# Attention of three more batches on 64x64 quarters of the array, with two casts moved ahead of value loads

## Chip, cores and metric

The kernel runs on one core of one Trainium2 chip. The metric is the time of one execution on the device in microseconds (us), median of several runs. A profile's span runs from the first to the last instruction and is some 1.7 us shorter than that run's time.

## The reference, cut to what matters

```python
# q, k, v: (8 batches, 8 heads, 576 tokens, 64), fp32
q_d, k_d, v_d = means of four neighbouring tokens          # 144 coarse tokens
out_d     = softmax(q_d k_d^T / 8) v_d, repeated 4 times
out_local = softmax(q k^T / 8 where |i - j| < 4) v         # a narrow band
x = (out_up + out_local) as (4608 tokens, 512)
h = x @ w_in                    # 512 -> 2048
return gelu(h) @ w_out          # 2048 -> 512
```

The two dense layers (called MoE here) run in nine blocks of 512 tokens. While block c runs, the attention of batch c+1 is woven into it, so that the matmuls of the layers fill the time in which attention waits for exponentials.

## The kernel before

Attention has two forms. `attn` uses the whole 128x128 array, with keys and values of two heads laid out in zero-padded blocks; it served batches 1 to 5. `attn_q` uses the array as four 64x64 quarters; it served batches 6 and 7. `BQ` is the first batch on quarters. `fill(n)` issues n matmuls of the dense layers. Cuts are marked.

```python
    BQ = 6
    ...
    def scores(b, p):                     # whole array: 12 matmuls for a pair of heads
        for hh in range(2):
            nc.tensor.matmul(out=sc[...144 wide], lhsT=kdz[:, p, hh, 0:128], rhs=qd[:, p, :], ...)
        for j in range(NW):               # NW = 10 windows
            nc.tensor.matmul(out=sc[...57 to 60 wide], lhsT=kb[:, p, j, :], rhs=(qT0 if b == 1 else xT_of(b, "qn"))[...], ...)
    ...
    def scores_q(b, p):                   # quarters: 28 matmuls for a pair of heads
        for c in range(2):
            for hh in range(2):
                for g in range(2):
                    nc.tensor.matmul(out=sc[HS[g], o:o + DH], lhsT=kdt[HS[hh], p, HS[c]],
                                     rhs=qd[HS[hh], p, DH * g:DH * g + DH], start=True, stop=True)
        for i in range(5):
            for hh in range(2):
                for g in range(2):
                    nc.tensor.matmul(out=sc[HS[g], o:o + RL[i]], lhsT=kt[HS[hh], p, k0:k0 + 64],
                                     rhs=qt[HS[hh], p, q0:q0 + RL[i]], start=True, stop=True)
    ...
    def prep_q(b):                        # VectorE, for quarters
        if b == BQ:
            ...                           # masks and constants, once
        nc.vector.tensor_reduce(out=kdt, in_=kt...)           # sums of the keys
        nc.vector.tensor_reduce(out=qd, in_=qt...)            # sums of the queries
        ...                               # 8 copies of coarse keys into KE
        v_two(...); v_two(...); v_two(...)                    # sums of the values
        ...                               # 4 copies into v_d, 4 products into v_lm
    def attn_q(b, fill):
        fill(5)
        s_lo_q(b); scores_q(b, 0); exps_q(0)
        fill(11)
        for p in range(NP):               # NP = 4 pairs of heads
            av_q(b, p)
            if p + 1 < NP:
                scores_q(b, p + 1)
            norm_qa(p)
            ...
            else:
                fill(12)
    ...
    for c in range(NCH):                  # 9 blocks
        b = c + 1
        ...
        (prep_q if b >= BQ else prep)(b)
        ...
        f1()
        if b < B:
            (attn_q if b >= BQ else attn)(b, f2)
            if 1 < b < B - 2:
                v_load(b + 2)             # GpSimd: values, for two batches on
            if 1 < b < B - 3:
                qk_cast(b + 3)            # GpSimd: keys and queries to fp16 in DRAM
        f2()
        if 1 < b < B - 2:
            qk_turn(b + 2)                # SP: transposes from DRAM into SBUF
```

What the argument turns on stands between the lines: for every pair of heads a quarter form issues one burst of 76 small matmuls (28 of scores and 48 of averages), each with a weight load of its own (436 and 437 recorded for 438 matmuls in the stages of batches 6 and 7), and then 12 long matmuls of the dense layers.

## Time and profile before

| | before |
|---|---|
| median time | 323.03 us (321.87 to 323.53, 3 runs) |
| span of the profiled run | 321.2 us |
| TensorE busy | 98% of the span, 2850 matmuls |
| stage of batch 3 / 4 / 5 (whole array) | 33.43 / 32.69 / 32.70 us |
| stage of batch 6 / 7 (quarters) | 31.98 / 31.99 us |

A "stage" runs from the first matmul of a block to the first of the next, and I name it after the batch whose attention is in it.

### The profile page before, as it was taken

How to read it: one execution, taken by the hardware profiler on the slowest of the kernel's cores; microseconds unless marked ns; L12 is line 12 of the kernel's file. 1: busy time of each engine (PE TensorE's matmuls, PEld its weight loads, DVE VectorE, ACT ScalarE, POOL GpSimd, SP SyncE). 2: the span in 40 equal slices, each digit the busy share in tenths (PEclk: the TensorE clock that was granted, in tenths of full speed). 3: DMA queues.
4: the chain of work that ended last, by engine and by line, in shares of the span. 5: the costliest groups of instructions: out<-in, count | busy, mean ns of one | idle time of the engine just before them, and what ended most of it. 6: DMA issues, size and time to landing. Idle time of an engine off the chain costs nothing.

```text
span 321.2 us, 6933 instructions
## 1 busy us (share of the span) xinstructions
PE 313.4 (98%) x2850; PEld 166.0 (52%) x2850; DVE 184.3 (57%) x408; ACT 222.0 (69%) x385; POOL 116.3 (36%) x143
## 2 busy tenths in 40 slices
PE   8899999999999999999999999999999999999995
PEld 4775556544564455445544554455445544444444
DVE  6887576628883978891789177946792540000001
ACT  7887558876887687768876787767776777415610
POOL 8965849431847704922931645300000000000000
PEclk9999999999999999999999999999999999999999
DMA  6999999999999999999999999971200020020011
GB/s 79 163 202 158 148 175 177 165 137 206 95 171 160 187 179 151 162 219 161 149 211 189 155 155 223 168 89 37 100 0 2 35 101 0 4 96 33 2 65 65
DMA packets 155486, 39.96 MB, mean 124 GB/s; under 512 B 137408, under 2 KB 150976, under 8 KB 155456
## 3 DMA queue, kind: packets, MB, share of 16 engines
q0 software_dynamic: 122096, 23.02, 88.7%
q1 hardware_dynamic: 33360, 16.52, 28.1%
q8 instruction: 22, 0.36, 0.5%
q14 instruction: 8, 0.07, 0.1%
HBM read 46.01 MB, written 16.52 MB: 195 GB/s over the span
## 4 chain that ended last, share of the span: by engine, by line
PE 77%; DMA 10%; DVE 8%; ACT 3%; POOL 1%; issue 1%; DVEq 0%; POOLq 0%
PE m_ps L296 32%; PE m_ps L265 26%; DMA q_nat<-q 4%; DMA k_nat<-k 4%; PE m_first L255 4%; DMA q_nat<-in_q_dram 2%; DVE qd L321 2%; PE nm L579 2%; PE sc L569 1%; PE sc L551 1%; DVE kb L310 1%; PE m_ps L287 1%; PE m_ps L277 1%; PE sc L467 1%; DVE kdt L317 1%; DVE v_two L375 1%
## 5 line engine op out<-in xcount | busy, mean ns | idle before, releaser
L296 PE MATMUL m_ps<-w_out_sb,gT 128*128 128x512 f16 x544 | 126.6, 379 | 0.0
L265 PE MATMUL m_ps<-xT,w_in_sb 128*128 128x512 f16 x504 | 112.0, 379 | 0.1
L268 ACT ACTIVATE gT<-m_ps 128x512 f16<-128x512 f32 x126 | 75.2, 597 | 34.5 <-PE m_ps L265 34.5
L265 PEld LDWEIGHTS <-w_in_sb 128*128 128x128 f16 x504 | 48.6, 98 | 58.2 <-issue 1.6
L296 PEld LDWEIGHTS <-gT 128*128 128x128 f16 x544 | 49.9, 98 | 53.6
L145 POOL DMA_DIRECT2D v_win<-in_v_dram x40 | 31.3, 853 | 40.6 <-DMA v_grp<-in_v_dram 12.6
L291 DVE COPY out_sb<-m_ps 128x256 f32<-128x256 f32 x2 | 0.9, 426 | 54.4 <-PE m_ps L287 54.4
L300 ACT COPY out_sb<-m_ps 128x512 f32<-128x512 f32 x21 | 12.3, 585 | 23.8 <-PE m_ps L296 23.7
L594 DVE TENSOR_TENSOR xl<-nm,lr 128x576 f16<-128x576 f32 x20 | 15.2, 758 | 18.0 <-ACT lr L590 18.0
L609 DVE TENSOR_TENSOR xT<-xl,up 128x576 f16<-128x576 f16 (+8 forms) x41 | 22.1, 565 | 0.8
L737 POOL DMA_DIRECT2D v_win<-in_v_dram x20 | 13.6, 697 | 24.1 <-PE m_ps L265 10.9
L563 DVE TENSOR_TENSOR e<-e,band 128x576 f16<-128x576 f16 x20 | 9.1, 453 | 14.7 <-ACT e L558 14.6
L255 PE MATMUL m_first<-xT,w_in_sb 128*128 128x512 f16 x68 | 16.3, 379 | 0.0
L168 POOL DMA_DIRECT2D q<-in_q_dram x6 | 16.0, 2660 | 0.4 <-DMA w_out_sb<-in_moe_w_out_dram 0.4
L260 ACT ACTIVATE gT<-m_first 128x1024 f16<-128x1024 f32 x8 | 8.2, 1024 | 8.6 <-PE m_first L255 7.5
L589 ACT ACTIVATE lr<-lr 128x576 f32<-128x576 f32 x20 | 13.7, 683 | 0.6
L310 DVE COPY kb<-k_nat 64x2304 f16<-64x2304 f16 x8 | 8.2, 1020 | 10.1 <-DMA k_nat<-k 10.0
L168 POOL DMA_DIRECT2D k<-in_k_dram x6 | 13.3, 2216 | 1.4 <-DMA v_win<-in_v_dram 1.1
L557 ACT ACTIVATE ed<-sc 128x288 f16<-128x288 f32 x20 | 8.2, 408 | 7.8 <-PE sc L551 7.8
L588 ACT ACTIVATE lr<-sc 128x576 f32<-128x576 f32 x20 | 13.1, 656 | 0.5 <-PE sc L569 0.5
L558 ACT ACTIVATE e<-sc 128x576 f16<-128x576 f32 x20 | 12.9, 644 | 0.0
L155 POOL DMA_DIRECT2D v_grp<-in_v_dram x7 | 12.3, 1764 | 0.0
(234 smaller groups left out, 490.5 us busy)
## 6 DMA issues: line engine op xcount, KB each, us to landing
out_dram<-out_sb SPq DMA_DIRECT2D x35, 256.0 KB, 5.7
v_grp<-in_v_dram POOLq DMA_DIRECT2D x7, 512.0 KB, 16.0
k<-in_k_dram POOLq DMA_DIRECT2D x6, 576.0 KB, 12.8
q<-in_q_dram POOLq DMA_DIRECT2D x6, 576.0 KB, 15.7
v_win<-in_v_dram POOLq DMA_DIRECT2D x40, 72.0 KB, 9.7
w_in_sb<-in_moe_w_in_dram POOLq DMA_DIRECT2D x4, 512.0 KB, 9.0
w_out_sb<-in_moe_w_out_dram POOLq DMA_DIRECT2D x4, 512.0 KB, 9.6
v_win<-in_v_dram POOLq DMA_DIRECT2D x20, 64.0 KB, 8.1
```

Of the source, the lines that this page charges most:

```text
L145: nc.gpsimd.dma_start(out=vw[64 * hh:64 * hh + 64, 0:9, p, 64 * hh:64 * hh + 64], in_=bass.AP(x.tensor, x.offset, [[D, 64], [57 * D, 9], [ ...
L168: nc.gpsimd.dma_start(out=t, in_=(k if nm == "kn" else q)[b].rearrange("h s d -> s h d"))
L255: nc.tensor.matmul(out=half[j], lhsT=w_in_sb[:, fc, 128 * j:128 * j + 128], rhs=xT[:, fc, x0:x0 + 512], start=(fc == 0), stop=(fc == 3))
L265: nc.tensor.matmul(out=ps, lhsT=w_in_sb[:, fc, 128 * j:128 * j + 128], rhs=xT[:, fc, x0:x0 + 512], start=(fc == 0), stop=(fc == 3))
L268: nc.scalar.activation(out=g[:, j, :], in_=ps, func=ACTF.Gelu)
L296: nc.tensor.matmul(out=ps, lhsT=g[:, j, 128 * t:128 * t + 128], rhs=w_out_sb[:, j, :], start=(j == 0), stop=(j == NJ - 1))
L558: nc.scalar.activation(out=e.rearrange("p (g c) -> p g c", g=2), in_=sc2[:, :, 0:SH], func=ACTF.Exp, scale=0.125)
L588: nc.scalar.activation(out=lr2, in_=sc2[:, :, 0:SH], func=ACTF.Ln)
L589: nc.scalar.activation(out=lr2, in_=lr2, func=ACTF.Exp, scale=-1.0)
L594: nc.vector.tensor_tensor(out=xl.rearrange("p (g c) -> p g c", g=2), in0=nm2[:, :, 0:SH], in1=lr2, op=ALU.mult)
L609: nc.vector.tensor_tensor(out=xT[:, p, y:y + z - a].rearrange("p (g r) -> p g r", r=4), in0=xl[:, a:z].rearrange("p (g r) -> p g r", r=4), ...
L737: nc.gpsimd.dma_start(out=quarter(b)["vw"][HS[g], i, :, :], in_=v[b, :, w:w + 64, :].rearrange("h s d -> s h d"))
```

## The change

Its intent: the quarter form took 31.98 us for a stage against 32.7 on the whole array, so batches 3, 4 and 5 should use it too. The casts of batch 6 move ahead of the value loads of batch 5, so that they do not come late.

```diff
-    BQ = 6
+    BQ = 3
@@ in the loop over blocks
             (attn_q if b >= BQ else attn)(b, f2)
+            if b == 3:
+                qk_cast(6)
             if 1 < b < B - 2:
                 v_load(b + 2)
-            if 1 < b < B - 3:
+            if b in (2, 4):
                 qk_cast(b + 3)
```

## The prediction

> **What bounds the kernel now.** I read the page's busy table and slices first, then the waits, then one call of busy time by stage, then the timeline of the two stages that matter.
>
> ```profile
> PE 313.4 (98%) x2850; PEld 166.0 (52%) x2850; DVE 184.3 (57%) x408; ACT 222.0 (69%) x385; POOL 116.3 (36%) x143
> PEclk9999999999999999999999999999999999999999
> DMA  6999999999999999999999999971200020020011
> ```
>
> TensorE works 98% of the span at full clock, so time comes off only by giving it less to do, or is lost by making it wait. The DMA engines are as full until about 225 us (slice 28 of 40), so a late transfer is the first thing to fear.
>
> I cut the run at the first matmul of each 512-token block. While block c runs, the attention of batch c+1 is woven into it: batches 3, 4, 5 in the first three rows, 6 and 7 (already on quarters) in the next two, none in the last.
>
> ```profile
> core 0: us, PE busy (x) PEld busy (x) DVE busy (x) ACT busy (x) POOL busy (x), PEclk, DMA share, GB/s
> 99.33:132.76 33.43, 32.85 (x246) 17.27 (x244) 24.60 (x41) 25.71 (x47) 19.31 (x20) 1.00 1.80 168
> 132.76:165.45 32.69, 32.69 (x245) 17.21 (x244) 22.26 (x42) 25.61 (x47) 18.10 (x21) 1.00 1.83 183
> 165.45:198.15 32.70, 32.70 (x245) 17.20 (x244) 22.15 (x45) 25.62 (x47) 13.21 (x16) 1.00 1.90 178
> 198.15:230.13 31.98, 31.98 (x438) 15.65 (x436) 22.06 (x59) 23.05 (x39) 3.78 (x6) 1.00 0.81 110
> 230.13:262.12 31.99, 31.99 (x438) 15.69 (x437) 20.19 (x44) 23.16 (x39) 0.00 (x0) 1.00 0.09 35
> 262.12:289.79 27.67, 27.67 (x130) 12.52 (x130) 0.80 (x2) 11.94 (x21) 0.00 (x0) 1.00 0.10 38
> ```
>
> The two forms stand side by side over the same MoE work: 27.67 us bare, 32.70 with attention on the whole array, 31.98 on quarters. Attention costs 5.03 us in one form and 4.31 in the other. All rows but the first have no idle TensorE. In the first row 0.58 us is idle, and the timelines of VectorE and TensorE show why:
>
> ```profile
> 103.62 2.83 DVE L310 COPY kb<-k_nat 64x2304 f16<-64x2304 f16 x1 [3.87 <-DMA k_nat<-k]
> 111.41 2.55 DVE L321 TENSOR_REDUCE qd<-q_nat 128x576 f16<-128x2304 f16 x1
> 117.51 0.97 DVE L563 TENSOR_TENSOR e<-e,band 128x576 f16<-128x576 f16 x2
> ...
> 118.01 0.41 PE L569 MATMUL sc<-e,ON 128*128 128x288 f16 x2 [0.57 <-DVE e L563]
> ```
>
> Batch 3 comes late: VectorE is idle 3.87 us until the transposed keys land, runs its preparation from 103.62 to 117.5 without a pause, masks, and TensorE, which was free at 117.44, starts at 118.01. So in this stage VectorE and the transposes behind it set the pace, not TensorE. In the next two stages the preparation ends 5 us ahead of the mask.
>
> [...] The 20 score matmuls and 8 coarse ones on quarters take 0.36 us in all (216.75 to 217.11), against 0.42 for 12 whole-array ones, though each record lasts about 190 ns in both; and 11 MoE matmuls ahead of a quarter group take 2.48 us where 11 at 216 ns (12.12 us over 56) are 2.38, so a switch costs about 0.10. [...] the key copy at 103.62 took 2.83 us where the same copy at 133.10 took 0.75, while GpSimd was issuing the query cast from 103.12 to 105.86. [...] The transposes (12.5 and 12.9 us to landing for batch 3) run beside the value loads and casts, with both queues' shares adding to 1.80 in the first row above.
>
> **The change part by part.**
>
> 1. TensorE, batches 3, 4 and 5. Per batch, four pairs: whole array 0.42 (scores) + 0.79 (averages, 88.14 to 88.93) = 1.21 each, 4.84, plus 0.25 for the coarse tail: 5.09. Quarters: 0.50 (216.25 to 216.75) + 0.36 + 0.10 switch = 0.96 each, 3.84, plus 0.34 for the tail: 4.2. That agrees with the stage table, which I use: 32.70 − 31.98 = **0.72** for batch 5, 32.69 − 31.98 = **0.71** for batch 4. All of it is on the path, since TensorE has no idle time there.
>
> 2. Batch 3, which VectorE paces. Taken off VectorE: the four key-block copies (2.83 + 0.48 + 0.77 + 0.17, 4.3 us in the chain), 0.9 of copies of the coarse keys, and the tail maximum. Put on it: the once-only set-up of masks and constants, which moves here from batch 6 (198.58 to 200.84 there, 2.27 us). It fits into the 3.87 us of waiting, if nothing blocks it. Then the keys' sums 103.62 to 106.2. Then the queries' sums, which in the kernel before never had to wait, because the copies came first; now they do. The queries' transpose is issued at 96.84 and takes 12.9 us: 109.74. In batch 6 the queries' sums start at 203.31 and the last preparation ends at 211.73: 8.42 us. So 109.8 + 8.42 = 118.2, plus a mask of 0.46 and a 0.05 hand-over: TensorE could start its averages at **118.7**. It would be there at 113.17 + 4.25 (212.00 to 216.25 in batch 6) = 117.42, so it waits 1.3 us instead of 0.57. From there to the end of the stage batch 6 takes 13.88 (216.25 to 230.13): 132.58 against 132.76 before. **Gain 0.18**: the faster array runs into the transpose.
>
> 3. ScalarE: a quarter pair takes two logs and exponentials of 0.77 + 0.80 in place of 0.66 + 0.68 + 0.41 + 0.44, so less. Not on the path in either form.
>
> 4. Value loads of 3, 4 and 5: ten transfers of 64 KB in place of eight of 72 and two of 32, both 640 KB and 5120 runs of 128 bytes. Median landing 8.1 us against 9.7 and 12.5. Neutral.
>
> 5. The order of the casts. Batch 6's casts come after batch 5's value loads now (issued 155.14 and 156.84) and would be at about 132. They reuse batch 4's scratch, and the query one must wait for the transpose of 122.62 + 13.3 = 136. The 1.15 MB go ahead of the values of batch 5, so the last of these are issued at about 158 instead of 154.7 and land, with 9 us, at 167. They are wanted at about 181 (183.4 now, less 2). The group values are wanted for sums at about 171 and should land by 156 (issued near 138, 16 to 18 us). In return the casts of 6 and 7 come up to 20 and 8 us sooner. Neither side waits in the trace before, so it is worth **0**, unless it saves the change from a wait.
>
> 6. Set-up leaves batch 6: its preparation ended at 211.73 and its first mask ran at 215.48, so 0.
>
> Sum: 0.18 + 0.71 + 0.72 = 1.61 us. 323.03 − 1.61 = **321.4 us**.
>
> **The rivals.**
>
> *Full gain.* The transposes of batch 3 land 1.3 us or more sooner, because the quarter-form loads beside them finish faster (8.1 against 9.7 us). Then the wait before the first averages vanishes, the stage falls to 31.98, and the sum is 1.45 + 0.71 + 0.72 = 2.9: 320.1 us. For it: those medians. Against: the same bytes in the same short runs, on engines that are full.
>
> *The set-up is locked out.* Its small copies and memsets at 99.7 meet GpSimd issuing values (98.94 to 101.1), then the two casts (to 105.86). If they are held to 105.9 as the key copy was, the keys' sums run 106 to 108.6, still ahead of the queries at 109.74. It costs nothing up to about 1 us later, and then one for one. At worst, up to the end of the group-value issue at 106.9 with copies left, 1 us: 322.4.
>
> *DMA becomes the bound.* The queries land later, or the casts of 6 delay the transposes of 5 or the values. For batch 3 each us costs one. For batch 5 the queries land at 163 now (149.76 + 13.3); the preparation needs 8.4 us after them and the mask is at about 182, so about 10 us are free; batch 4 has about 8, batch 6 about 9 and batch 7 over 10. All three late at once would give 324 or more. Against: the total bytes don't change and the two later casts gain room.
>
> *The quarter form meets its own chain.* Its masks end 0.05 us before TensorE needs them (219.76 for 219.81), so a slower mask would cost up to 0.1 for each of nine pairs. Batches 3 to 5 have the same order of work, so I put 0.2 on this.
>
> **Range and chances.** The two quiet batches carry 1.43 with hardly any doubt. Batch 3 is worth −1.3 to +1.45 around 0.18. Runs of the kernel before spread 1.7 us (321.87 to 323.53), so a median may be off by 0.5. Range **319.8 to 323.2**. Over 2% needs 6.5 us, more than double what everything together could give (2.9): 0.01. Slower by 2% needs several late transfers at once: 0.02. Within 2%: 0.97.
>
> **What would show it right or wrong.** Stages of batches 4 and 5 of 31.98 with no idle TensorE (step 1). In batch 3's stage, VectorE waiting before the queries' sums for a transpose, and TensorE's one wait before its first averages, about 1.3 us, on the mask (step 2); no wait would mean the full gain, over 2.5 us would mean late transposes or lock-out, told apart by what ended VectorE's idle time and by whether small copies last over 1 us. Casts of batch 6 issued from about 132 to 136 and batch 5's values without a waiting TensorE (step 5). A wait in any later stage on a transpose or value load would make the prediction wrong.

## More of the kernel before

The busy table and the table by stage stand in the prediction. One further part of the page, the DMA queues (packets, MB, share of 16 engines' span), was read over when I predicted:

```profile
q0 software_dynamic: 122096, 23.02, 88.7%
q1 hardware_dynamic: 33360, 16.52, 28.1%
q8 instruction: 22, 0.36, 0.5%
```

The first queue is what GpSimd issues, the second what SP issues. The third brings instructions: 22 packets of 16 KB at half a per cent of the share. It looks like nothing, and no one would read a cost from its share.

## The result and the profile after

| | before | after |
|---|---|---|
| median time | 322.56 us (321.87 to 323.53, 4 runs) | 332.28 us (331.67 to 333.27, 4 runs) |
| span profiled | 321.2 us | 330.0 us |
| mean granted clock | 0.999 | 0.99 |

The kernel before has one run more here than in the table above. The ratio is 1.0302, with a 95% interval of 1.0262 to 1.0343: slower by 3%. Ratios here and below are the mean time of one kernel's fast runs over that of the other's fast runs in the same rounds, so not quite the ratio of the medians quoted. Executions over 1.5% slower than the fastest of the same kernel are left out of the means.

The page of the kernel after (busy us, share, instructions; clock in 40 slices; one DMA queue):

```profile
PE 314.9 (95%) x3426; PEld 163.0 (49%) x3426; DVE 178.7 (54%) x417; ACT 214.6 (65%) x361; POOL 114.0 (35%) x143
...
PEclk9999999999999979999979999999999999999999
...
q8 instruction: 27, 0.44, 0.6%
```

TensorE is busy for 1.5 us more and for a smaller share, so it waits. Two slices show a clock of 0.7. The 576 matmuls and as many weight loads that came in are five more packets of instructions.

By stage (batches 3, 4, 5, 6, 7), to be held against the rows in the prediction. The DMA share is the summed time of all packets over the time of 16 engines, so it can pass 1:

```profile
core 0: us, PE busy (x) PEld busy (x) DVE busy (x) ACT busy (x) POOL busy (x), PEclk, DMA share, GB/s
...
99.02:137.90 38.88, 33.88 (x438) 16.66 (x436) 22.20 (x60) 23.15 (x39) 21.38 (x20) 0.96 1.74 172
137.90:174.78 36.88, 33.93 (x437) 16.20 (x437) 20.77 (x44) 23.36 (x39) 14.47 (x19) 0.95 1.84 173
174.78:206.87 32.09, 32.09 (x438) 15.73 (x437) 23.04 (x47) 23.14 (x39) 12.92 (x15) 1.00 1.54 163
206.87:238.85 31.98, 31.98 (x437) 15.69 (x437) 20.17 (x44) 23.14 (x39) 4.17 (x7) 1.00 0.68 89
238.85:270.83 31.98, 31.98 (x437) 15.67 (x437) 20.18 (x44) 23.14 (x39) 0.00 (x0) 1.00 0.10 35
```

Batch 5 did what was expected of it: 32.09 against 32.70. All the loss is in two stages: batch 3 took 5.45 us more than before and batch 4 took 4.19 more. What TensorE waited for over the whole span (us in total, times, longest), the largest waits but for one at start-up that both kernels have:

```profile
PE sc L439 <- issue: 2.9, 1, 2.9
PE sc L467 <- DVE e L456: 2.4, 1, 2.4
PE sc L445 <- issue: 1.4, 1, 1.4
...
PE nm L467 <- issue: 1.2, 1, 1.2
```

The second is the wait for the mask in batch 3 that the prediction spoke of, at 2.4 us in place of 1.3. The other three say "issue": nothing that the profile records held TensorE up. They lie in the middle of rows of equal small matmuls, which is odd. On TensorE's timeline the largest reads so (start, us, line, what, how many, and in brackets the idle time before):

```profile
160.42 2.76 PE L296 MATMUL m_ps<-w_out_sb,gT 128*128 128x512 f16 x12
...
163.62 0.23 PE L439 MATMUL sc<-qd,kdt 64*64 64x72 f16 x5
166.79 0.22 PE L439 MATMUL sc<-qd,kdt 64*64 64x72 f16 x3 [2.95 <-issue]
166.80 0.37 PE L445 MATMUL sc<-q_nat,k_nat 64*64 64x58 f16 x20
167.10 4.44 PE L296 MATMUL m_ps<-w_out_sb,gT 128*128 128x512 f16 x12
```

Five of eight coarse score matmuls run, then nothing for 2.95 us, then the other three, though all eight have the same operands at hand. After it, 12 dense matmuls take 4.44 us instead of 2.76. The clock record is at half speed from 167.12 to 170.54, for 3.41 us, which costs 1.7 us. The same follows the wait at 119.55 (half speed from 119.34 to 122.75). So a silent stop is paid twice when the clock drops.

The sum closes. A stage without trouble is 31.98. Batch 3: 38.88 − 31.98 = 6.90, against 2.36 (mask) + 1.7 (half clock) + 1.42 + 1.22 (two silent gaps) = 6.7. Batch 4: 36.88 − 31.98 = 4.90, against 2.95 + 1.7 = 4.65.

**What the silent gaps are.** I numbered TensorE's instructions in program order (weight loads, matmuls and the uncounted ones), laid the trace's records on them, and looked at the number at which each gap begins. The queue of instructions moved 0.44 MB for 6875 of them, which is 64 bytes each, in 27 packets of 16 KB: pages of 256 instructions. What follows is my own working from the trace, not a view of the profile:

```
gap in the kernel after                     number mod 256   page landed   idle ends, after landing
125.16 -> 126.77  L445, 10th of 20               195           125.48            1.28 us
133.47 -> 134.88  L467                           195           133.28            1.60 us
163.65 -> 166.79  L439, 6th of 8                 195           165.25            1.54 us
116.81 -> 119.55  L467 (the mask wait)           145             -                 -
```

(Here times are starts of the matmuls on either side, and the number is that of the matmul that came late.) All three silent gaps begin at the same place in a page and end 1.3 to 1.6 us after a page has come. The wait for the mask begins elsewhere. So the reading is that TensorE had run out of instructions. The DMA view shows the page that ended the large gap. First from 158 to 164.3, then the microsecond after it:

```profile
q0 software_dynamic: 2527, 0.46, 88.1%
q1 hardware_dynamic: 1647, 0.64, 58.6%
```

```profile
q0 software_dynamic: 361, 0.18, 134.1%
q8 instruction: 1, 0.02, 5.8%
q1 hardware_dynamic: 15, 0.00, 3.4%
```

For 6.3 us no page came, while values, casts and transposes kept the engines full (88 + 59%, more than one transfer in flight for each). In a quiet stretch, from 222.3 to 223.3, the page is alone:

```profile
q8 instruction: 1, 0.02, 6.1%
```

When is a page asked for? The trace does not say. In the quiet stages of batches 6 and 7, before and after, the transfer starts 0.9 to 1.4 us after TensorE reaches about number 150 of a page, for 12 pages of 13; I take that as the mark of the request. That is an inference, and a rough one: the thirteenth page, due amid dense matmuls, started 4.0 us after the mark though the DMA engines were quiet. From the mark to the place where TensorE ran dry are some 300 instructions. How long these last is the runway (my working, from the same records):

| where | mark, us | transfer starts after | runway | landed before running dry | gap |
|---|---|---|---|---|---|
| after, batch 3, quarters | 119.6 | 4.36 | 5.60 | −0.33 | yes |
| after, batch 3, quarters | 125.0 | 7.16 | 8.51 | 0.19 | yes |
| after, batch 4, quarters | 151.4 | 5.38 | 8.33 | 2.02 | no |
| after, batch 4, quarters | 157.4 | 6.90 | 6.23 | −1.60 | yes |
| after, batch 5, quarters | 193.2 | 4.26 | 6.81 | 1.57 | no |
| after, batch 6, quarters, quiet | 222.3 | 1.00 | 6.66 | 4.68 | no |
| before, batch 3, whole array | 131.9 | 5.71 | 22.27 | over 14 | no |
| before, batch 4, whole array | 151.7 | 9.20 | 19.61 | over 8 | no |

Pages came just as late in the kernel before, up to 9.2 us after the mark, but a page lasted about 20 us there. In a stretch of quarter attention it lasts 5.6 to 8.5 in this table (4.4 at the least, in batch 6). The quiet stages needed pages as often, but got them 0.9 to 1.4 us after the mark, 12 times of 13. The gaps of this table came where both met: a short runway (5.60 to 8.51 us) and full DMA engines (the transfer 4.36 to 7.16 us after the mark). Since a landed page took 1.3 to 1.6 us here until its first instruction ran, a margin under that made a gap.

### The profile page after: what moved, and what is told of

It reads as the page before. It is cut to its first block, busy times and chain, and to the rows that moved or that the text cites.

```text
span 330.0 us, 8096 instructions
## 1 busy us (share of the span) xinstructions
PE 314.9 (95%) x3426; PEld 163.0 (49%) x3426; DVE 178.7 (54%) x417; ACT 214.6 (65%) x361; POOL 114.0 (35%) x143
## 4 chain that ended last, share of the span: by engine, by line
PE 84%; DMA 6%; DVE 3%; ACT 2%; issue 2%; POOL 1%; DVEq 0%; POOLq 0%
PE m_ps L296 35%; PE m_ps L265 29%; DMA q_nat<-q 4%; PE m_first L255 4%; DMA q_nat<-in_q_dram 2%; PE sc L467 2%; PE nm L467 2%; PE sc L445 1%; PE m_ps L287 1%; PE m_ps L277 1%; DVE qd L404 1%; PE nm L579 1%; PE sc L551 1%; POOL k_nat L183 1%; PE sc L569 1%
## 5 line engine op out<-in xcount | busy, mean ns | idle before, releaser
L296 PE MATMUL m_ps<-w_out_sb,gT 128*128 128x512 f16 x544 | 127.9, 385 | 0.0
L296 PEld LDWEIGHTS <-gT 128*128 128x128 f16 x544 | 50.9, 99 | 58.2 <-issue 3.3
L737 POOL DMA_DIRECT2D v_win<-in_v_dram x50 | 35.7, 834 | 56.4 <-PE nm L467 16.3
L501 ACT ACTIVATE lr<-sc 128x720 f32<-128x720 f32 x20 | 15.4, 770 | 27.6 <-PE sc L467 24.0
L502 ACT ACTIVATE lr<-lr 128x720 f32<-128x720 f32 x20 | 16.1, 803 | 0.6
L145 POOL DMA_DIRECT2D v_win<-in_v_dram x16 | 12.3, 878 | 9.7 <-DMA q<-in_q_dram 4.1
L168 POOL DMA_DIRECT2D k<-in_k_dram x6 | 14.4, 2393 | 1.6 <-DMA v_win<-in_v_dram 1.4
L404 DVE TENSOR_REDUCE qd<-q_nat 128x576 f16<-128x2304 f16 x5 | 12.7, 2544 | 3.6 <-DMA q_nat<-q 3.6
L403 DVE TENSOR_REDUCE kdt<-k_nat 128x576 f16<-128x2304 f16 x5 | 12.7, 2546 | 2.7 <-DMA v_win<-in_v_dram 2.7
L467 PE MATMUL nm<-e,v_win 64*64 64x58 f16 (+1 forms) x400 | 10.5, 193 | 1.2 <-issue 1.2
```

The lines of the kernel that those rows point to most:

```text
L168: nc.gpsimd.dma_start(out=t, in_=(k if nm == "kn" else q)[b].rearrange("h s d -> s h d"))
L296: nc.tensor.matmul(out=ps, lhsT=g[:, j, 128 * t:128 * t + 128], rhs=w_out_sb[:, j, :], start=(j == 0), stop=(j == NJ - 1))
L404: nc.vector.tensor_reduce(out=qd, in_=qt.rearrange("p a (g r) -> p a g r", r=4), axis=AX.X, op=ALU.add)
L467: nc.tensor.matmul(out=out(g, hh), lhsT=lhsT(g, hh), rhs=rhs(g, hh), start=start, stop=stop)
L501: nc.scalar.activation(out=lr2, in_=sc2[:, :, 0:SH + DH], func=ACTF.Ln)
L502: nc.scalar.activation(out=lr, in_=lr, func=ACTF.Exp, scale=-1.0)
```

## The experiments

**The theories.** Fetch: TensorE's pages of instructions come late where quarters use them fast and the DMA engines are full. Rivals: the new order of casts delays transfers; the quarter form stops by itself (its mode of tiling, or its own chain of exponentials and masks); the whole loss comes from batch 3's late queries, with the rest following. Medians of the kernel before lay at 322.6 to 322.9 us.

### The order and the form apart

The old order of casts with `BQ = 3`:

```diff
 (to the kernel before)
-    BQ = 6
+    BQ = 3
```

> Quarter form for batches 3 to 5 with the casts of batch 6 left where they were. Fetch theory (TensorE runs out of instructions because its 16 KB instruction pages queue behind data transfers; 256 instructions a page): the order of the casts matters little, the silent gaps of 1 to 3 us stay in some stage of batches 3 to 5, and the time stays at 328 to 335 us. Order theory (moving 1.15 MB of casts ahead of the values is what hurts): the gaps and the loss vanish, 321 to 323 us.

Measured: 331.92 us (330.15 to 332.94), ratio 1.0268 (1.0208 to 1.0327). TensorE's timeline has no wait for the mask here, but

```profile
128.11 0.37 PE L445 MATMUL sc<-q_nat,k_nat 64*64 64x58 f16 x11 [4.44 <-issue]
...
169.75 0.22 PE L439 MATMUL sc<-qd,kdt 64*64 64x72 f16 x3 [2.66 <-issue]
```

both at number 195 of a page, both ended by one that had landed 1.3 to 1.4 us before. (The two rows are of two stretches of that timeline; a third gap at number 195, of 0.33 us, stands at 163.00.) The order isn't the cause. Nor is the wait for the mask, since the loss is there without it.

The new order with the old form:

```diff
 (to the kernel before)
+            if b == 3:
+                qk_cast(6)
             if 1 < b < B - 2:
                 v_load(b + 2)
-            if 1 < b < B - 3:
+            if b in (2, 4):
                 qk_cast(b + 3)
```

> Whole-array form for batches 3 to 5 with the new order of the casts. Fetch theory: no silent gap, since a whole-array batch uses some 490 TensorE instructions where a quarter one uses 876; 321 to 324 us. Order theory: the loss of 8 to 10 us is here, 330 us or more.

Measured: 322.97 us over 12 runs, ratio 0.9999 (0.9973 to 1.0025), no silent gap. The order is worth nothing either way.

Only batch 5 changes its form, in the old order:

```diff
 (to the kernel before)
-    BQ = 6
+    BQ = 5
```

> Quarter form for batch 5 alone, old order. My first sum: 0.7 us less than before, 321.9. Fetch theory: that, if no page comes late while batch 5 runs, or 1.5 to 4.5 us more than before if one does, with the gap at the same remainder (195) of the instruction's number by 256. So between 321 and 327, and whichever it is, the trace has to show the gap or its absence.

Measured: 325.03 us over 20 runs, ratio 1.0061 (1.0039 to 1.0083). Batch 5, which gained in the full change, lost here: its stage took 34.25 us, with gaps of 0.55 and 1.36 us idle, at 188.97 and 195.44. Both begin at number 195, and end 1.38 and 1.44 us after a page. So the full change had luck in batch 5; there the page had landed 1.57 us before it was too late. One batch of quarters under load was enough.

### The pages themselves

If gaps begin where pages end, moving the pages must move the gaps. 32 tiny matmuls in the start-up, 64 instructions, do nothing else to the stages:

```diff
 (to the kernel after)
     spin(10)
+    ps = ppool.tile([128, 512], F32, tag="tr", name="spin")
+    for _ in range(32):
+        nc.tensor.matmul(out=ps[:, 0:8], lhsT=zt[:, 0:128], rhs=zt[:, 0:8], start=True, stop=True)
     warm()
```

> The changed kernel with 32 tiny matmuls more (64 instructions) in the prologue, long before the stages in question. Fetch theory: every silent gap again begins at remainder 195 of the instruction's number by 256, which is now another place in the program: 64 instructions earlier, so no longer at the tenth score matmul of batch 3's third pair or the sixth coarse one of batch 4's last. Form theory (the quarter form itself stumbles over a buffer or a bank at those places): the gaps stay at the same matmuls, at remainder 3. Time 328 to 335 in either case.

Measured: 330.95 us (2 runs), ratio 1.0239 (1.0199 to 1.0279). No gap was left at the old places. The new ones:

```profile
132.19 0.22 PE L445 MATMUL sc<-q_nat,k_nat 64*64 64x57 f16 x3 [3.43 <-issue]
...
196.50 0.35 PE L445 MATMUL sc<-q_nat,k_nat 64*64 64x58 f16 x19 [1.76 <-issue]
```

They begin at other matmuls of the program and again at number 195 of their page, and end 1.41 and 1.45 us after one landed. Batch 4 lost its gap and took 32.29 us, batch 5 got one and took 34.02. A fault of the quarter form would have stayed at its matmuls, and a wait for data has no reason to begin at the same number of a page wherever that page falls. This is the plainest proof of the fetch theory.

Next the load. The value loads of batches 4 and 5 and the casts of 5 and 6 are left out, with older data in their place, so the output is wrong:

```diff
 (to the kernel after)
             if b == 3:
-                qk_cast(6)
-            if 1 < b < B - 2:
+                for nm in ("kn", "qn"):
+                    v16[nm, 5], v16[nm, 6] = v16[nm, 3], v16[nm, 4]
+            if b == 4 or b == 5:
                 v_load(b + 2)
-            if b in (2, 4):
+            if b == 4:
                 qk_cast(b + 3)
```

> The changed kernel without the value loads of batches 4 and 5 and without the casts of 5 and 6 (old data used again, the result is wrong on purpose), so that few data transfers run beside batches 3 and 4 from about 106 us on. Fetch theory: instruction pages start within about 2 us of being asked for instead of 4 to 7, no silent gap in batch 4 and at most one in batch 3, batch 4's stage back to about 32.0 us; in all 324 to 327 us, as the wait for batch 3's mask is untouched. Form theory: gaps and time as they were, 330 us or more.

Measured: 322.89 us over 12 runs, ratio 1.0007 (0.9982 to 1.0032). By stage, batches 3, 4 and 5:

```profile
97.85:133.52 35.67, 33.72 (x438) 16.19 (x436) 21.89 (x60) 23.04 (x39) 6.56 (x6) 0.95 1.34 159
133.52:165.60 32.08, 32.08 (x438) 15.71 (x437) 20.35 (x44) 23.14 (x39) 4.03 (x6) 1.00 0.47 92
165.60:197.93 32.33, 32.19 (x438) 15.88 (x438) 23.54 (x47) 23.38 (x39) 13.12 (x16) 1.00 1.58 147
```

The same instructions with fewer transfers: no page gap at all, pages 1.1 to 3.1 us after the mark in batches 3 and 4, and some 9 us of the loss gone (7.8 of it in these three stages; the two profiles differ by 1.2 us ahead of them, where both kernels do the same). That is more than I had expected. What is left in the first row is the wait for the mask (1.95 us idle, ahead of 117.96) and the half clock after it (118.96 to 122.37). So the two losses are separate.

The other way round: whole-array attention as before, with 48 useless quarter matmuls over zeros ahead of the scores of each pair of batches 3 to 7. This adds bursts of instructions, but not the quarter form.

```diff
 (to the kernel before)
+    def burst(sc):
+        for i in range(48):
+            r, c = HS[i % 2], HS[i // 2 % 2]
+            nc.tensor.matmul(out=sc[c, 512 * (i % 2):512 * (i % 2) + 58], lhsT=zt[r, 0:64], rhs=zt[r, 0:58], start=True, stop=True)
...
+        if b > 2:
+            burst(sc)        # in scores; in scores_q without the condition
```

> The kernel before, with 48 tiny matmuls on 64x64 tiles, over zeros, put ahead of the scores of every pair of batches 3 to 7; no data moves otherwise. Their own work is about 0.65 us each time, 13 us in all: 335 us if nothing else happens. Fetch theory: besides that, silent gaps of 1 to 4 us at remainder 195 in batches 3 to 5, where transfers fill the DMA engines, and none in batches 6 and 7, where there are even more TensorE instructions per us but few transfers; 337 to 348 us. Form theory: no gap in batches 3 to 5, as the attention there has the whole-array form; 335 us.

Measured: 339.91 us (2 runs), ratio 1.0517 (1.0476 to 1.0557). On TensorE's timeline:

```profile
130.43 0.20 PE L587 MATMUL nm<-e,v_win 128*128 128x60 f16 x1 [2.63 <-issue]
...
159.46 0.40 PE L587 MATMUL nm<-e,v_win 128*128 128x57 f16 x8 [2.30 <-issue]
```

The gaps now stand in whole-array matmuls, at number 195 again, 1.43 to 1.45 us after a page. Where no gap came, the burst cost 2.53 us a stage (batch 5: 35.23 against 32.70) and 1.64 in batches 6 and 7. Batch 3 took 37.93, that is 35.30 busy and 2.63 of gap; batch 4 took 39.22, that is 35.23 + 2.30 + 1.7 of half clock. So neither the quarter form nor its chain is needed for a gap, only many instructions in a short time (the burst itself runs on 64x64 tiles, but the gaps stand among whole-array matmuls); in batches 6 and 7, with a DMA share of 0.59 and 0.10 (1.79 and 1.86 in batches 3 and 4), the same bursts made none.

The last of this kind loads the DMA engines where they had been quiet: eight useless casts after the attention of batches 5 and 6, in the kernel before.

```diff
 (to the kernel before)
+            if b == 5 or b == 6:
+                if b == 6:
+                    nc.gpsimd.tensor_copy(out=hold, in_=st[NP - 1]["xl"][0:1, 0:1])
+                for i in range(4):
+                    t = dpool.tile([S, H, D], F16, tag=f"junk{b}{i}", bufs=1, name="junk")
+                    nc.gpsimd.dma_start(out=t, in_=(k, q)[i % 2][b].rearrange("h s d -> s h d"))
```

> The converse of the light kernel: the kernel before, with eight useless casts more (four after the attention of batch 5, four after that of 6), so that transfers fill the DMA engines while batches 6 and 7, on quarters since ever and never late, run. Nothing waits for them. Fetch theory: silent gaps of 1 to 3 us at remainder 195 appear in the stages of batches 6 and 7, one or two in each, and those stages rise from 32.0 to 33.5 to 36 us; 326 to 331 us in all. If the late pages need something of batches 3 to 5 other than the transfers, both stages stay at 32.0 and the time at 323.

Measured: 326.92 us (4 runs), ratio 1.0118 (1.0064 to 1.0172). Batch 6, which had never had a gap, had one:

```profile
230.02 0.22 PE L467 MATMUL nm<-e,v_win 64*64 64x57 f16 x3 [2.01 <-issue]
```

It begins at number 194, and the page had landed 1.59 us before its end. Batch 7 had none and took 32.03 us: when its pages were asked for, at 254 and 258, the useless casts had ended, and the pages came in 1.1 us. So half of what I expected came, and the other half was a fault of my timing.

Over all 14 profiles, TensorE was idle for more than 0.15 us 21 times between 60 and 300 us without another engine or a transfer that ended the wait. All 21 begin at number 194 or 195 of a page.

### The wait ahead of batch 3's mask

The queries' sums come second in VectorE's preparation and wait for the transpose. Twice I moved them back.

Queries last:

```diff
 (to the kernel after, in prep_q)
             nc.vector.tensor_reduce(out=kdt, ...)
-            nc.vector.tensor_reduce(out=qd, ...)
 ...
+            nc.vector.tensor_reduce(out=qd, ...)     # after copies, value sums, v_d and v_lm
```

> The changed kernel with the sums of the queries put last in VectorE's preparation. If the 2.4 us wait for the first mask of batch 3 comes from the query transpose landing at 110.5 with 8.4 us of preparation behind it, that wait vanishes, and with it the 3.4 us at half clock that follow (worth 1.7): 4 us less, 328 us, the other gaps staying. If the half clock does not come from the gap, it stays and only 2.4 us go: 330. If VectorE's preparation is not what the mask waits for, nothing changes: 332.

Measured: 332.52 us (4 runs), ratio 1.0295 (1.0243 to 1.0348): a miss, as I had expected 328. Values first, then keys and queries:

```diff
 (to the kernel after, in prep_q: the order of the same work)
-  keys, queries, KE copies, values, v_d and v_lm
+  values, v_d and v_lm, keys, queries, KE copies
```

> The changed kernel with VectorE's sums of the values put ahead of those of keys and queries, so that they run while it waits for the transposes of batch 3. The second try at the mask's wait: after the queries land (about 110.5) only 2.5 us of sums and 0.8 of copies are left, so the first mask is done by about 116.5 and TensorE, there at about 117.2, doesn't wait; with the wait goes the half clock that follows it, 4 us in all: 328 us, the gaps for instructions staying. If the wait was not that chain, 332.

Measured: 331.28 us (4 runs), ratio 1.0258 (1.0208 to 1.0309): a miss too. What TensorE waited for, first with the queries last, then with the values first (the start-up waits and smaller ones left out):

```profile
PE sc L446 <- issue: 3.2, 1, 3.2
PE sc L440 <- issue: 2.1, 1, 2.1
PE nm L468 <- issue: 1.8, 1, 1.8
PE sl L427 <- DVE qd L419: 1.7, 1, 1.7
```

```profile
PE sc L439 <- issue: 3.2, 1, 3.2
PE nm L467 <- issue: 2.3, 1, 2.3
PE sc L445 <- issue: 2.3, 1, 2.3
...
PE sl L426 <- DVE e L418: 0.8, 1, 0.8
```

In both the wait ahead of the mask is gone, turned into a shorter one ahead of the coarse scores. In both the page gaps are longer in sum than in the kernel after (7.2 and 7.8 us against 5.6), and batch 5 has one as well. What they won on the mask, they lost on pages.

So I tried both cures at once: the light load (wrong) with the values first and the queries last.

```diff
 (to the kernel of the light load, in prep_q: the order of the same work)
-  keys, queries, KE copies, values, v_d and v_lm
+  values, v_d and v_lm, keys, KE copies, queries
```

> The light kernel (no value loads of 4 and 5, no casts of 5 and 6, wrong on purpose) with VectorE's value sums ahead of the transposes and the queries' sums last. If the late instruction pages and the wait for batch 3's mask, each with its half clock, are all that stands between the prediction and the measurement, then with both out of the way the three stages are near 32.0 us each, as the prediction's first step had it, and the time is 3.6 us below the light kernel's: 319 to 320 us, ratio to before about 0.99. If something else in the quarter form costs time in these batches, a stage stays at 33 us or more.

Measured: 324.12 us over 20 runs, ratio 1.0049 (1.003 to 1.0068), a miss. The mask's wait was gone, and batch 4 took 32.08. But TensorE waited twice for the queries' sums, 2.1 us in all, and had one page gap of 1.4 us. The sums were late since a copy that now met GpSimd took far longer (VectorE's timeline):

```profile
169.22 0.34 DVE L407 COPY v_d<-v_lm 64x512 f16<-64x512 f16 x1
...
169.89 4.11 DVE L407 COPY v_d<-v_lm 64x512 f16<-64x512 f16 x1
```

GpSimd issued two casts from 169.34 to 173.89; the copy ended at 174.00. In batch 3 the same copy took 2.51 us beside another issue. The prediction noted the same of the key copy (2.83 us for 0.75). Whether the issues on GpSimd are the cause is not shown, as I ran nothing that takes them away.

### Two attempts at a better kernel

Value sums of batch 3 ahead of its transposes, on the kernel before:

```diff
 (to the kernel before, in prep)
+        if b == 3:
+            v_down(b)
 ...
-        v_down(b, (0, 1) if b == 2 else (0, 1, 2))
+        if b != 3:
+            v_down(b, (0, 1) if b == 2 else (0, 1, 2))
```

> A candidate: the kernel before, whole-array form and old order, with the value sums of batch 3 alone moved ahead of its transposes, into the 3.9 us in which VectorE waits. The wait of 0.6 to 0.95 us before batch 3's averages vanishes, nothing else changes: 0.5 us less than before, ratio 0.998, the stage at 32.7.

Measured: 322.91 us over 14 runs, ratio 0.9996 (0.9969 to 1.0023). In the profiled run the stage of batch 3 took 32.70 us without its wait. But that wait comes and goes by itself: 0.57 us in the profiles of before and of `BQ = 5`, none with the new order alone. (The 0.95 of my expectation is the time from one matmul's start to the next, about the same in both.) A gain of 0.1% is below what these rounds resolve.

On top of that, `BQ = 5` with the DMA engines kept quieter under batch 5: the casts of 7 go ahead of the values of 6, and the values of 6 and 7 are held until the attention of 5 and 6 is done.

```diff
 (to the kernel of the value sums)
-    BQ = 6
+    BQ = 5
...
-            if 1 < b < B - 2:
+            if b > 4:
+                nc.gpsimd.tensor_copy(out=hold, in_=st[NP - 1]["xl"][0:1, 0:1])
+            if 1 < b < 4:
                 v_load(b + 2)
-            if 1 < b < B - 3:
                 qk_cast(b + 3)
+            elif 4 < b < B - 1:
+                v_load(b + 1)
...
+        if b == 3:
+            qk_cast(7)
```

> A candidate built on the fetch theory: the same, with quarters for batch 5 too, and the transfers moved out of the way of its attention: the casts of batch 7 go ahead of the values of 6, and the values of 6 and 7 are held until the attention of 5 and 6 is done. If pages are late only beside transfers, batch 5's stage has no silent gap and falls from 32.7 to 32.0 or 32.1, and the time is 1.2 us below before: ratio 0.996. If the gaps stay (batch 5 alone cost 2 us with the old order) the ratio is over 1.004.

Measured: 324.80 us over 18 runs, ratio 1.0058 (1.0039 to 1.0078), a miss. The casts of 7 were still in flight when batch 5's page was due: GpSimd's queue had 135.8% of 16 engines' share from 183.8 to 188.3. So there was a gap of 0.82 us ahead of 190.65, at number 195, and batch 6 waited 0.7 us for its held values. No version here beats the kernel before.

## Why the prediction was wrong

I said 321.4 us and 0.97 for within 2%; it was 332.28, slower by 3%.

**Step 1 failed: "All of it is on the path, since TensorE has no idle time there."** The size was right wherever pages came in time: batch 5 gained 0.61 us for a predicted 0.72, and batch 4 took 32.08 under the light load for a predicted 31.98. What was wrong was to carry a stage time from a quiet place to a loaded one. The 31.98 came from rows with a DMA share of 0.81 and 0.09, the rows it went to had 1.83 and 1.90. Both figures stood in the table that I printed, and so did the matmul counts, 438 for 245. I asked of the DMA engines only whether data would come late. The pages of instructions come as DMA packets too (0.5% of the 16 engines' share before), and came later where the engines were full: in the table above their transfers started 4.26 to 9.20 us after the mark, and 1.00 us in quiet. I had not counted them as a load. Measured, this is 1.42 + 1.22 us of gaps in batch 3 and 2.95 + 1.7 (half clock) in batch 4, 7.3 us together.

**Step 2 had the right mechanism and the wrong size.** VectorE did wait for the queries, then the mask held TensorE up (VectorE's timeline of the kernel after):

```profile
104.39 2.55 DVE L403 TENSOR_REDUCE kdt<-k_nat 128x576 f16<-128x2304 f16 x1 [2.66 <-DMA v_win<-in_v_dram]
110.53 2.55 DVE L404 TENSOR_REDUCE qd<-q_nat 128x576 f16<-128x2304 f16 x1 [3.59 <-DMA q_nat<-q]
...
119.03 0.46 DVE L456 TENSOR_TENSOR e<-e,band 128x576 f16<-128x576 f16 x1
```

The set-up fitted ahead of the keys, as predicted. The queries' sums began at 110.53, not 109.8; the preparation then took 8.50, not 8.42; TensorE was there at 117.2, not 117.42. The wait was 2.36 us instead of 1.3. I left out what follows it: 3.41 us of half clock, 1.7 us more. Without the page gaps the stage would take 31.98 + 2.36 + 1.7 = 36.0 us against 33.43 before: a gain of 0.18 became a loss of some 2.6. Nor is the wait a fixed one: in the profiles of the old order and of the shifted pages, with the same preparation, TensorE did not wait for the mask. There its stage began at 101.18 and 102.65 instead of 99.02, and the queries' sums at 110.11 and 111.62.

**Steps 3, 4 and 6** held: ScalarE never paced a stage, and no wait of TensorE ended on a value load. **Step 5** held: the order alone has ratio 0.9999.

**The rivals.** "DMA becomes the bound" named the right engines and, at 324 or more, the right direction. But it looked at keys, queries and values only. "The quarter form meets its own chain" did not occur: but for batch 3, TensorE waited for no mask. "Full gain" did not come: the queries' sums began later than predicted, not sooner. "The set-up is locked out" did not come in the profile of the change, where its ten copies of the band mask took 1.04 us, but in those of the old order and of the shifted pages they took 4.95 and 4.99 us while GpSimd issued the casts, and the keys' sums began only at 107.64 and 109.15. No wait of TensorE came of it there. None of the four spoke of instructions, and the range was narrow because all four shared that blind spot. My 0.02 for slower asked for "several late transfers at once"; that is what came, in a queue I had not read.

**What stays open.** Which of the other queues delays a page most was not separated: the light load took away both casts and value loads. That a page is asked for at about number 150 is inferred. Why the clock falls after one idle stretch and not after another was not tested: in the kernel with bursts, 2.63 us of idle time in batch 3 was not followed by half clock (the stage's clock was 1.00), and 2.30 us in batch 4 was (0.96).

## What to carry to other kernels

Count the instructions of the engine that bounds the kernel per microsecond, not only its busy time: many small ones use up fetched pages fast (some 300 instructions lasted 5.6 to 8.5 us on quarters under load here, and about 20 us on the whole array), and a page came late where the DMA engines were full (its transfer started 4.26 to 9.20 us after the mark, against 0.9 to 1.4 for 12 pages of 13 in quiet). Before carrying the time of a form from one stage to another, compare the DMA share of both: the form with two and a half times the matmuls (about 310 for 117 in a stage here, without the 128 of the dense layers) took 31.98 us a stage at shares of 0.68 and 0.10, but 32.09 at 1.54 and 36.88 at 1.84. A wait marked "issue" in a row of equal instructions is a hint to number them and look at the instruction queue.
